# Attention backward: q for dK in 32 small pieces issued by the sync engine, three more buffers of transposed e, and dV four units later

## The chip, the cores and the metric

One core of a Trainium2 chip. The metric is device microseconds (us) of one execution; lower is better. A run more than 1.5% above the fastest of its kernel in the same rounds counts as slow and is left out of the ratios.

## The reference, cut to what matters

The program computes the forward of two attention layers and all eight gradients. The change touches the backward of layer B: softmax attention with 16 heads of 28 channels, 2048 queries and keys, and one k and one v shared by all heads.

```python
# x [1,2048,448]; wq [448,448]; wk, wv [448,28]; wo [448,448]; all bf16
q = (x @ wq).reshape(B, S, 16, 28).transpose(0, 2, 1, 3)
k = x @ wk                      # shared by the 16 heads
v = x @ wv
p = softmax(einsum("bhqd,bkd->bhqk", q, k) * 28 ** -0.5)
o = einsum("bhqk,bkd->bhqd", p, v)
# backward with dS = p * (dP - D):  dV = sum_h p^T dO, dK = sum_h dS^T q, dQ = dS k
```

Nine outputs: the forward and eight gradients.

## The kernel before

The main loop has 512 units. A block is 8 units: two heads and 256 queries against all 2048 keys, 64 blocks in all; a unit is 256 keys of it. A unit does 128x512 tiles twice: scores on PE, exp on ACT (eT, keys on partitions), the gradient product on DVE and, through a copy by ACT, on POOL (dsT), and a 32x32 transpose on DVE (dsx). After the 512 units come 28 of drain, then the projections of the gradients.

dV needs e with the queries on partitions. So every second unit the sync engine (SP) issues one DMA transpose of 512 KB, eN from eT: 256 in all. dK needs q with the queries on partitions (qX), four times over, at partitions 0, 32, 64 and 96. q lies in DRAM (qn_d); POOL fetches it for the next 8 blocks in four loads of 256 KB.

```python
pn_ = cs_.enter_context(tc.tile_pool(name="ceN", bufs=11, side="right"))
pq_ = cs_.enter_context(tc.tile_pool(name="cqX", bufs=2, side="right"))
# ... in the loop over u:
if u in (2, 4, 6, 8) or u % 64 in (30, 38, 46, 54) and u < 448:
    qc, a = (u // 64 + 1, (u % 64 - 30) // 8) if u > 20 else (0, (u - 2) // 2)
    if a == 0:
        qX[qc] = pq_.tile([P, 4, 2, 512], BF16, name="qX")
    nc.gpsimd.dma_start(qX[qc][32 * a:32 * a + 32, :, :, :]..., qn_d[qc * 256:(qc + 1) * 256, :]...)
if u == 4:
    nc.vector.memset(oTs[64:128, :], 0.0)
# ...
nc.scalar.activation(out=et[:, u % 2, 1, :], in_=sp[1][:, :], func=ACT.Exp, scale=scale)
if u % 2 == 1:
    en = pn_.tile([P, 16, P], BF16, name="eN")
    nc.sync.dma_start_transpose(en[:, :, :], et[:, :, :, :].rearrange("p a b c -> p (a b c)"))
    eN[u // 2] = en
if u % 2:
    b, i = divmod(u - 27, 8)          # dK of block b, units 8b+27 .. 8b+33
    ...
else:
    o_dq((u - 2, u - 1), (u - 20, u - 19))
    for n in {2: (0,), 4: (1, 2), 6: (3,)}.get(u % 8, ()):
        if 0 <= (b := u // 8 - 2) < NB:
            dv_mm(b, n // 2, n % 2)   # a quarter of dV: 4 matmuls of 512 columns
```

Of the kernel before, what the change touches and what calls it, by code (L numbers as in the profile page):

```python
# [11 lines left out]
BF16 = mybir.dt.bfloat16  # L12
F32 = mybir.dt.float32
# [3 lines left out]
D = 448  # L17
P = 128
# [6 lines left out]
def kernel(  # L25
# [21 lines left out]
    nc = tc.nc  # L47
    S = A_x.shape[1]
# [17 lines left out]
    R2 = R2x[:, 1:NS + 1, :]  # L66
    R3 = reg.tile([P, 4, 1408], BF16, name="R3")
    R4 = reg.tile([P, 4, 512], BF16, name="R4")
    qn_d = dpool.tile([S, 512], BF16, name="qn_d")
    on_d = dpool.tile([S, 512], BF16, name="on_d")  # L70
    wqT_d = dpool.tile([512, D], BF16, name="wqT_d")
    wkvT_d = dpool.tile([64, D], BF16, name="wkvT_d")
# [439 lines left out]
    def phase_B_pre(pa, cA, awk, psA, io):  # L512
        xbT, wq_pad, rep, bsel, qn, sh = io
        kT, vT, vaug, kn, qT = kT_rep, vT_rep, vaug_, kn_, R1

        def gen(shape, dt=F32):
            return psA.tile(shape, dt, name="agen")

        ones16 = cA.tile([P, H], BF16, name="ones16")
        nc.gpsimd.memset(ones16[:], 1.0)  # L520
        nc.gpsimd.memset(ones16[0:1, :], 0.0)
        neg = cA.tile([P, 1], F32, name="neg")
        nc.gpsimd.memset(neg[:], 0.0)
        for j in range(4):
            nc.gpsimd.memset(neg[32 * j:32 * j + 1, :], -1.0)
        kmx = cA.tile([H, NQC], F32, name="kmx")
        sqk = []
        def k_max(qc, sq):
            ps = gen([H, 512])
            mm(ps[:, :], ones16[0:32, :], sq[0:32, :])  # L530
            nc.vector.tensor_reduce(out=kmx[:, qc:qc + 1], in_=ps[:, :], axis=AX.X, op=ALU.max)

        prev = None
        for qc in range(NQC):
            for w, dst in [(0, kT), (1, vT)]:
                ps = gen([P, 512])
                for c in range(4):
                    mm(ps[:, :], rep[:, w, c, :], xbT[:, c, qc * 512:(qc + 1) * 512], start=(c == 0), stop=(c == 3))

                if w:  # L540
                    nc.vector.tensor_scalar(out=dst[:, qc * 512:(qc + 1) * 512], in0=ps[:, :], scalar1=neg[:, 0:1],
                                            scalar2=None, op0=ALU.add)
                else:
                    nc.scalar.activation(out=dst[:, qc * 512:(qc + 1) * 512], in_=ps[:, :], func=ACT.Identity,  # L544
                                         bias=neg[:, 0:1])
            sq = awk.tile([P, 512], BF16, name="osb")
            nc.vector.tensor_tensor(out=sq[0:32, :], in0=kT[0:32, qc * 512:(qc + 1) * 512],  # L547
                                    in1=kT[0:32, qc * 512:(qc + 1) * 512], op=ALU.mult)
            if prev is not None:
                k_max(qc - 1, prev)  # L550
            prev = sq
        shifts = [flat(sh)[0:H, i * 512:(i + 1) * 512] for i in range(NQC - 1)] + [flat(R3)[0:H, 5120:5632]]
        kmax2 = cA.tile([H, 1], F32, name="kmax2")
        for qc in range(NQC):
            qs = slice(qc * 512, (qc + 1) * 512)
            pn = psA.tile([P, 512], F32, name="aacc")
            sqs = []
            for g in range(6):
                if qc == 0 and g == 2:
                    k_max(NQC - 1, prev)  # L560
                    nc.vector.tensor_reduce(out=kmax2[:], in_=kmx[:], axis=AX.X, op=ALU.max)
                if g < 4:
                    ps = gen([P, 512])
                    for c in range(4):
                        mm(ps[:, :], wq_pad[:, c, g * P:(g + 1) * P], xbT[:, c, qs], start=(c == 0), stop=(c == 3))
                    nc.scalar.activation(out=qT[:, g, qs], in_=ps[:, :], func=ACT.Copy)
                    sq = awk.tile([P, 512], BF16, name="osb")
                    nc.vector.tensor_tensor(out=sq[:, :], in0=qT[:, g, qs], in1=qT[:, g, qs], op=ALU.mult)
                    sqs.append(sq)
                if g >= 2:  # L570
                    mm(pn[:, :], bsel[:, g - 2, :], sqs[g - 2][:, :], start=(g == 2), stop=(g == 5))
            shift = shifts[qc]
            nc.scalar.activation(out=shift, in_=pn[0:H, :], func=ACT.Sqrt, scale=kmax2[:, 0:1])
            for g in range(4):
                nc.gpsimd.dma_start(qT[:, g, qs].rearrange("(j r) s -> j r s", r=32)[:, 0, :], shift[4 * g:4 * g + 4, :])
            if qc % 2:
                q2 = slice((qc - 1) * 512, (qc + 1) * 512)
                t2 = slice(4 * qc - 4, 4 * qc + 4)
                for g in range(4):
                    nc.sync.dma_start_transpose(qn[:, t2, g * P:(g + 1) * P], qT[:, g, q2])  # L580
                nc.sync.dma_start(qn_d[q2, :].rearrange("(t p) c -> p t c", p=P), qn[:, t2, :])
        for w, dst in [(1, vaug_), (0, kn_)]:
            ps = gen([P, NS, 32])
            for st in range(NS):
                for c in range(4):
                    mm(ps[:, st, :], xbT[:, c, st * P:(st + 1) * P], rep[:, w, c, 0:32], start=(c == 0), stop=(c == 3))
            nc.vector.tensor_copy(out=dst, in_=ps[:])
        nc.gpsimd.memset(vaug_[:, :, 0:1], 1.0)
# [13 lines left out]
    NB = 64  # L602
# [4 lines left out]
    with ExitStack() as cs_:  # L607
        psA = psc.enter_context(tc.tile_pool(name="psAcc", bufs=1, space=bass.MemoryType.PSUM))
        pe_ = cs_.enter_context(tc.tile_pool(name="ceT", bufs=10, side="right"))
        pn_ = cs_.enter_context(tc.tile_pool(name="ceN", bufs=11, side="right"))  # L610
        pd_ = cs_.enter_context(tc.tile_pool(name="cdsT", bufs=5, side="right"))
        px_ = cs_.enter_context(tc.tile_pool(name="cdsx", bufs=2, side="right"))
        pq_ = cs_.enter_context(tc.tile_pool(name="cqX", bufs=2, side="right"))
# [45 lines left out]

        identF = pp_.tile([P, P], F32, name="identF", bufs=1)  # L660
        make_identity(nc, identF[:])
        oTs = pm_.tile([P, 256], F32, name="oTs", bufs=1)
        wo = pp_.tile([P, 4, D], BF16, name="wo", bufs=1)
        oTq = {}

# [32 lines left out]
            nc.scalar.activation(out=t, in_=src, func=ACT.Copy, scale=0.0)  # L698

        def post_load(k):  # L700
            if k in (2, 4, 6, 8):
                zero(post["dkvT"][64:128, 256 * k - 512:256 * k])
            if k == 0:
                mix = pq_.tile([P, 4, 2, 512], BF16, name="qX").rearrange("p a b c -> p (a b c)")
                post["dkvT"], post["dkvn"], post["wkvT"] = mix[:, 0:2048], mix[:, 2048:3072], mix[:, 3072:3072 + D]
                zero(post["wkvT"][64:128, :])
                nc.sync.dma_start(post["wkvT"][0:64, :], wkvT_d[:, :])
            i = k % 4
            rows = slice(i * 512, (i + 1) * 512)
            if k == 8:  # L710
                t = pe_.tile([P, 2, 2, 512], BF16, name="eT").rearrange("p a b c -> p (a b c)")
                post["wqT"] = t[:, 0:4 * D].rearrange("p (g c) -> p g c", c=D)
# [96 lines left out]
        def dk_m(b, m):  # L809
            qc, pair, g, hp = blk(b)  # L810
            h, B, s = m // 8, (m // 2) % 4, m % 2
            for a in range(4):
                rhs = dsx[b][32 * a:32 * a + 32, :, h, :, :].rearrange(
                    "p u t (b i s) -> p u t b i s", b=4, s=2)[:, :, :, B, :, s]
                mmt(dk_acc[32 * a:32 * a + 32, :],
                    qX[qc][32 * a:32 * a + 32, B, s, pair * 64 + 32 * h:pair * 64 + 32 * h + 32],
                    rhs, (32 * a, 32 * a), b == 0 and m == 0, b == NB - 1 and m == 15)

        def o_mm(v):
            b, tp = divmod(v, 8)  # L820
# [42 lines left out]
        with tc.manual_schedule():  # L863
            tc.keep_in_program_order(nc.scalar.activation(out=ex[:], in_=ex[:], func=ACT.Exp))
            for u in range(NU + 28):
# [23 lines left out]
                if hasD:  # L889
# [4 lines left out]
                    cp = pc_.tile([P, 512], BF16, name="cp")  # L894
                    nc.scalar.activation(out=cp[:, :], in_=dp[1][:, :], func=ACT.Copy)  # L895
                    nc.gpsimd.tensor_tensor(out=dst[:, 1, :], in0=cp[:, :], in1=ew[:, w % 2, 1, :], op=ALU.mult)  # L896
                if u in (2, 4, 6, 8) or u % 64 in (30, 38, 46, 54) and u < 448:
                    qc, a = (u // 64 + 1, (u % 64 - 30) // 8) if u > 20 else (0, (u - 2) // 2)
                    if a == 0:
                        qX[qc] = pq_.tile([P, 4, 2, 512], BF16, name="qX")  # L900
                    nc.gpsimd.dma_start(qX[qc][32 * a:32 * a + 32, :, :, :].rearrange("j b s c -> j b (s c)"),  # L901
                                        qn_d[qc * 256:(qc + 1) * 256, :].rearrange("(b j s) c -> j b (s c)", b=4, s=2))
                if u == 12:
                    nc.gpsimd.dma_start(wo, wo_d[:, 0:D].rearrange("(g p) c -> p g c", p=P))
                if u == 4:
# [25 lines left out]
                if hasS:  # L931
                    nc.scalar.activation(out=et[:, u % 2, 1, :], in_=sp[1][:, :], func=ACT.Exp, scale=scale)  # L932
                    if u % 2 == 1:
                        en = pn_.tile([P, 16, P], BF16, name="eN")
                        nc.sync.dma_start_transpose(en[:, :, :], et[:, :, :, :].rearrange("p a b c -> p (a b c)"))
                        eN[u // 2] = en

                if u % 2:
                    b, i = divmod(u - 27, 8)
# [2 lines left out]
                            dk_m(b, m)  # L942
                else:
                    o_dq((u - 2, u - 1), (u - 20, u - 19))
                    for n in {2: (0,), 4: (1, 2), 6: (3,)}.get(u % 8, ()):
                        if 0 <= (b := u // 8 - 2) < NB:
                            dv_mm(b, n // 2, n % 2)
                y = u - 18

                if 512 <= u < 530 and u % 2 == 0:  # L950
# [117 lines left out]
```

## Time and profile before

| | before |
|---|---|
| three timed runs, us | 1121.45, 1121.01, 1111.03 |
| profiled run: span, mean clock | 1111.3 us, 0.994 |
| first start of a transpose of e to the last | 802.7 us (235.3 to 1038.0) |

### The profile page before, as it was taken

Reading aid. Unit: us, or ns where it says so; the run is one execution under the profiler, and the core shown is the slowest. Engines: PE = TensorE matmul, PEld = TensorE weight load, DVE = VectorE, ACT = ScalarE, POOL = GpSimd, SP = SyncE. Lnnn points to the kernel's source line nnn. Section 1 sums busy time; section 2 is a strip of 40 time slices with the busy share of each in tenths; the row PEclk is TensorE's granted clock in tenths of the full one; section 3 lists DMA queues with packets and bytes.
Section 4 is the critical chain, followed back from the end, with each engine's and each line's share of the span. In section 5 each row is a group of like instructions: output and inputs, shape, how many; then the busy total and the mean of one; then the engine's idle time right before and its main releaser. Section 6 shows DMA issues by size and latency. Waiting matters only on the chain.

```text
span 1111.3 us, 42443 instructions
## 1 busy us (share of the span) xinstructions
PE 1047.9 (94%) x17280; PEld 503.6 (45%) x17285; DVE 893.8 (80%) x1773; ACT 876.6 (79%) x1744; POOL 768.7 (69%) x993
## 2 busy tenths in 40 slices
PE   9999999969999999999999999999999999999898
PEld 4545545435444444444444444444444444444344
DVE  7896400427999999999999999999999999999842
ACT  6454122548999999999999999999999999999521
POOL 6001252325888898898889888888898888888740
PEclk9999999979999999999999999999999999999999
DMA  9869899199999999999999999999999999999992
GB/s 264 147 128 185 166 174 222 43 202 198 177 167 184 195 196 177 187 189 187 191 186 199 191 183 197 195 188 178 191 193 180 195 182 194 192 184 184 237 212 62
DMA packets 674963, 202.89 MB, mean 183 GB/s; under 512 B 649760, under 2 KB 670288, under 8 KB 674768
## 3 DMA queue, kind: packets, MB, share of 16 engines
q1 hardware_dynamic: 662368, 177.03, 100.1%
q0 software_dynamic: 7440, 19.20, 6.7%
q10 hardware_dynamic: 4960, 3.96, 1.2%
q8 instruction: 135, 2.21, 0.8%
q14 instruction: 60, 0.49, 0.2%
HBM read 22.83 MB, written 14.77 MB: 34 GB/s over the span
## 4 chain that ended last, share of the span: by engine, by line
PE 65%; DVE 12%; DMA 10%; ACT 9%; issue 2%; SPq 1%; POOL 0%; DVEq 0%; ACTq 0%
PE dk_acc L627 18%; PE agen L81 12%; PE sps L627 11%; DMA eN<-eT 8%; ACT eT L932 7%; PE oq L627 6%; PE dps L627 5%; PE aacc L81 4%; DVE dsT L893 4%; PE dv_acc L627 3%; DVE dsx L964 3%; PE sps L81 3%; PE sps L800 1%; ACT cp L895 1%; DVE R L916 1%
## 5 line engine op out<-in xcount | busy, mean ns | idle before, releaser
L896 POOL TENSOR_TENSOR dsT<-cp,eT 128x512 bf16<-128x512 bf16 x512 | 590.0, 1157 | 108.7 <-ACT cp L895 96.8
L893 DVE TENSOR_TENSOR dsT<-dps,eT 128x512 bf16<-128x512 f32 x512 | 341.4, 667 | 27.9 <-PE dps L627 22.1
L627 PEld LDWEIGHTS <-R 32*128 32x128 bf16 (+1 forms) x8704 | 228.5, 94 | 296.7 <-issue 263.0
L964 DVE STREAM_TRANSPOSE dsx<-dsT 128x512 f32<-128x512 f32 x512 | 356.0, 696 | 2.1
L888 ACT ACTIVATE eT<-sps 128x512 bf16<-128x512 f32 x512 | 312.5, 610 | 42.8 <-PE dps L627 19.0
L895 ACT ACTIVATE cp<-dps 128x512 bf16<-128x512 f32 x512 | 313.5, 612 | 12.9 <-PE dps L627 11.9
L932 ACT ACTIVATE eT<-sps 128x512 bf16<-128x512 f32 x512 | 320.1, 625 | 0.0
L627 PE MATMUL dk_acc<-dsx,qX 32*32 32x512 bf16 x4096 | 268.0, 376 | 0.0
L627 PE MATMUL dps<-doT,R 32*128 32x256 bf16 x2048 | 248.0, 269 | 6.1 <-ACT cp L895 2.0
L627 PE MATMUL sps<-R,R 32*128 32x256 bf16 (+1 forms) x2240 | 226.4, 274 | 8.6 <-DVE R L858 1.9
L627 PE MATMUL oq<-eT,R 128*32 128x256 bf16 x2048 | 158.3, 275 | 0.0
L627 PE MATMUL oq<-dsT,R 128*32 128x256 bf16 x2048 | 156.4, 274 | 0.1
L627 PEld LDWEIGHTS <-qX 32*32 32x32 bf16 x4096 | 79.8, 89 | 114.5 <-issue 54.1
L627 PE MATMUL dv_acc<-eN,don 128*32 128x512 bf16 x1024 | 103.0, 379 | 9.9 <-DMA eN<-eT 9.7
L397 POOL MEMSET ga<- 64x448 bf16 x2 | 0.9, 470 | 93.4 <-DVE pr L348 80.4
L547 DVE TENSOR_TENSOR osb<-R 32x512 bf16<-32x512 bf16 x4 | 1.7, 414 | 63.1 <-ACT R L544 63.1
L81 PEld LDWEIGHTS <-R 128*128 128x128 bf16 (+1 forms) x361 | 29.5, 99 | 27.5 <-issue 5.6
L627 PE MATMUL sps<-identF,oTs 128*32 128x64 f32 x1024 | 27.6, 225 | 7.5 <-ACT eT L932 0.2
L627 PEld LDWEIGHTS <-don 128*32 128x32 bf16 x1024 | 34.4, 97 | 0.3
L774 POOL TENSOR_TENSOR onat<-oTs,rl 128x128 bf16<-128x128 f32 x64 | 25.7, 402 | 6.5 <-DVE rl L770 6.5
L901 POOL DMA_DIRECT2D qX<-qn_d x32 | 18.6, 581 | 16.5 <-DMA qn_d<-gaT 16.5
L81 PE MATMUL agen<-R,R 128*128 128x448 bf16 x128 | 28.6, 353 | 0.8 <-ACT R L220 0.6
(225 smaller groups left out, 1029.1 us busy)
## 6 DMA issues: line engine op xcount, KB each, us to landing
qX<-qn_d POOLq DMA_DIRECT2D x32, 256.0 KB, 5.5
eN<-eT SPq DMA_TRANSPOSE x256
out_dram<-osb ACTq DMA_DIRECT2D x22, 112.0 KB
qn_d<-gaT SPq DMA_DIRECT2D x2, 1024.0 KB
xa<-in_A_x_dram SPq DMA_DIRECT2D x8, 224.0 KB
ga<-in_grad_out_dram SPq DMA_DIRECT2D x4, 448.0 KB
xa<-in_grad_out_dram POOLq DMA_DIRECT2D x4, 448.0 KB, 8.9
out_dram<-wdq POOLq DMA_DIRECT2D x8, 224.0 KB, 5.2
```

The source lines that it names most:

```text
L81: nc.tensor.matmul(out_ap, lhsT=lhsT, rhs=rhs, start=start, stop=stop, tile_position=(0, 0))
L627: nc.tensor.matmul(out, lhsT=lhsT, rhs=rhs, start=start, stop=stop, tile_position=pos, skip_group_check=True)
L774: nc.gpsimd.tensor_tensor(out=onv, in0=os_, in1=r_[:].to_broadcast([P, 2, 2, 32]), op=ALU.mult)
L800: nc.tensor.transpose(tp2[q:q + 32, qb * P:(qb + 1) * P], don[b][:, qb, h, :], identB[:, :], tile_position=(0, q))
L888: nc.scalar.activation(out=et[:, u % 2, 0, :], in_=sp[0][:, :], func=ACT.Exp, scale=scale)
L893: nc.vector.tensor_tensor(out=dst[:, 0, :], in0=dp[0][:, :], in1=ew[:, w % 2, 0, :], op=ALU.mult)
L895: nc.scalar.activation(out=cp[:, :], in_=dp[1][:, :], func=ACT.Copy)
L896: nc.gpsimd.tensor_tensor(out=dst[:, 1, :], in0=cp[:, :], in1=ew[:, w % 2, 1, :], op=ALU.mult)
L901: nc.gpsimd.dma_start(qX[qc][32 * a:32 * a + 32, :, :, :].rearrange("j b s c -> j b (s c)"), qn_d[qc * 256:(qc + 1) * 256, :].rearrange("( ...
L916: nc.vector.tensor_scalar(out=qT_B[g][64 * hp:64 * hp + 64, qc * 256:(qc + 1) * 256], in0=oq[64:128, 0:256], scalar1=scale, scalar2=None, ...
L932: nc.scalar.activation(out=et[:, u % 2, 1, :], in_=sp[1][:, :], func=ACT.Exp, scale=scale)
L964: nc.vector.transpose(out=dsx[b][:, tp, :, :, :].rearrange("p h t c -> p (h t c)").bitcast(F32), in_=dsT[y][:, :, :].rearrange("p h c -> p ...
```

## The change

Its intent: give dV more slack against late transposes (due four units later, one quarter per even unit, and 14 buffers in place of 11 to keep eN that long). The room comes from q, held in pieces of four heads (2 KB per partition, not 8). That makes 32 pieces of four loads of 64 KB; all but the first two pieces are now issued by SP, between transposes. oTs also moves to another pool.

```diff
-    qn_d = dpool.tile([S, 512], BF16, name="qn_d")
+    qn_d = dpool.tile([4, S, P], BF16, name="qn_d")
@@ before the loop: two stores of 1 MB become eight of 256 KB
-        pn_ = cs_.enter_context(tc.tile_pool(name="ceN", bufs=11, side="right"))
+        pn_ = cs_.enter_context(tc.tile_pool(name="ceN", bufs=14, side="right"))
-        oTs = pm_.tile([P, 256], F32, name="oTs", bufs=1)
+        oTs = pp_.tile([P, 256], F32, name="oTs", bufs=1)
@@ new
+        def load_q(k, a, eng):
+            qc, g = divmod(k, 4)
+            if a == 0:
+                qX[k] = pq_.tile([P, 4, 2, P], BF16, name="qX")
+            eng.dma_start(qX[k][32 * a:32 * a + 32, :, :, :]..., qn_d[g, qc * 256:(qc + 1) * 256, :]...)
@@ in the loop
-                if u in (2, 4, 6, 8) or u % 64 in (30, 38, 46, 54) and u < 448:
-                    ... nc.gpsimd.dma_start(qX[qc]...)
+                if 2 <= u < 10:
+                    load_q((u - 2) // 4, (u - 2) % 4, nc.gpsimd)
@@ after the transpose of e, odd u
+                    k, a = divmod(u - 11, 16)
+                    if 2 <= k < 32 and a < 4:
+                        load_q(k, a, nc.sync)
@@ even u
-                    for n in {2: (0,), 4: (1, 2), 6: (3,)}.get(u % 8, ()):
-                        if 0 <= (b := u // 8 - 2) < NB:
-                            dv_mm(b, n // 2, n % 2)
+                    b, n = divmod(u - 22, 8)
+                    if 0 <= b < NB:
+                        dv_mm(b, n // 4, n // 2 % 2)
```

(Cut: the tiles of the drain, which took a q buffer before and now take eN buffers. The four loads of piece k are emitted one per unit, at units 16k+11 to 16k+14.)

More of the change, by code (lines that the diff above doesn't have):

```diff
@@ L580, in phase_B_pre @@
                     nc.sync.dma_start_transpose(qn[:, t2, g * P:(g + 1) * P], qT[:, g, q2])
-                nc.sync.dma_start(qn_d[q2, :].rearrange("(t p) c -> p t c", p=P), qn[:, t2, :])
+                    nc.sync.dma_start(qn_d[g, q2, :].rearrange("(t p) c -> p t c", p=P), qn[:, t2, g * P:(g + 1) * P])
         for w, dst in [(1, vaug_), (0, kn_)]:
@@ L700, in post_load @@
         def post_load(k):
-            if k in (2, 4, 6, 8):
-                zero(post["dkvT"][64:128, 256 * k - 512:256 * k])
-            if k == 0:
-                mix = pq_.tile([P, 4, 2, 512], BF16, name="qX").rearrange("p a b c -> p (a b c)")
-                post["dkvT"], post["dkvn"], post["wkvT"] = mix[:, 0:2048], mix[:, 2048:3072], mix[:, 3072:3072 + D]
+            if 5 <= k < 9:
+                zero(post["dkvT"][64:128, 512 * k - 2560:512 * k - 2048])
+            i = k % 4
+            rows = slice(i * 512, (i + 1) * 512)
+            if k == 4:
+                post["dkvT"], mix = (pn_.tile([P, 16, P], BF16, name="eN").rearrange("p a b -> p (a b)") for _ in range(2))
+                post["dkvn"], post["wkvT"] = mix[:, 0:1024], mix[:, 1024:1024 + D]
                 zero(post["wkvT"][64:128, :])
                 nc.sync.dma_start(post["wkvT"][0:64, :], wkvT_d[:, :])
-            i = k % 4
-            rows = slice(i * 512, (i + 1) * 512)
             if k == 8:
@@ L815, in dk_m @@
                 mmt(dk_acc[32 * a:32 * a + 32, :],
-                    qX[qc][32 * a:32 * a + 32, B, s, pair * 64 + 32 * h:pair * 64 + 32 * h + 32],
+                    qX[b // 2][32 * a:32 * a + 32, B, s, hp * 64 + 32 * h:hp * 64 + 32 * h + 32],
                     rhs, (32 * a, 32 * a), b == 0 and m == 0, b == NB - 1 and m == 15)
+        def load_q(k, a, eng):
+            qc, g = divmod(k, 4)
+            if a == 0:
+                qX[k] = pq_.tile([P, 4, 2, P], BF16, name="qX")
+            eng.dma_start(qX[k][32 * a:32 * a + 32, :, :, :].rearrange("j b s c -> j b (s c)"),
+                          qn_d[g, qc * 256:(qc + 1) * 256, :].rearrange("(b j s) c -> j b (s c)", b=4, s=2))
         def o_mm(v):
@@ L896 @@
                     nc.gpsimd.tensor_tensor(out=dst[:, 1, :], in0=cp[:, :], in1=ew[:, w % 2, 1, :], op=ALU.mult)
-                if u in (2, 4, 6, 8) or u % 64 in (30, 38, 46, 54) and u < 448:
-                    qc, a = (u // 64 + 1, (u % 64 - 30) // 8) if u > 20 else (0, (u - 2) // 2)
-                    if a == 0:
-                        qX[qc] = pq_.tile([P, 4, 2, 512], BF16, name="qX")
-                    nc.gpsimd.dma_start(qX[qc][32 * a:32 * a + 32, :, :, :].rearrange("j b s c -> j b (s c)"),
-                                        qn_d[qc * 256:(qc + 1) * 256, :].rearrange("(b j s) c -> j b (s c)", b=4, s=2))
+                if 2 <= u < 10:
+                    load_q((u - 2) // 4, (u - 2) % 4, nc.gpsimd)
                 if u == 12:
```

## The prediction

> **What bounds the kernel now.** I read the busy table first, then the stretches of the main loop (512 units, one 128x512 score pair each, then 28 units of drain), then the waits, then the timeline around the longest of them. Two stretches of the loop (columns: window, length, then busy us of PE, weight load, DVE, ACT, POOL, clock, DMA share, GB/s):
>
> ```profile
> 600.00:700.00 100.00, 95.44 (x1931) 44.58 (x1929) 96.37 (x186) 98.10 (x197) 88.95 (x105) 1.00 1.20 190
> 700.00:800.00 100.00, 93.47 (x1853) 42.92 (x1852) 92.74 (x177) 94.17 (x189) 86.07 (x103) 1.00 1.19 189
> ```
>
> Four engines are above 86%: they are coupled through three score banks and two gradient banks, and where nothing disturbs them ACT reaches 98%. The second window is worse by 2 to 4 us on every engine at once, so something outside them stops all of them. The waits over the loop name two candidates:
>
> ```profile
> ACT eT L888 <- PE sps L627: 17.8, 12, 9.8
> DVE dsT L893 <- PE dps L627: 17.8, 35, 1.9
> POOL qX L901 <- DMA qn_d<-gaT: 16.5, 1, 16.5
> DVE oTs L906 <- DMA qn_d<-gaT: 9.9, 1, 9.9
> PE dv_acc L627 <- DMA eN<-eT: 9.7, 10, 1.7
> ```
>
> First, PE waits ten times for the transposed e (eN) that dV reads. The timeline of the longest wait shows what one costs:
>
> ```profile
> 526.66 0.39 PE L627 MATMUL dv_acc<-eN,don 128*32 128x512 bf16 x3
> ...
> 528.71 0.38 PE L627 MATMUL dv_acc<-eN,don 128*32 128x512 bf16 x1 [1.66 <-DMA eN<-eT]
> ...
> 529.45 0.60 ACT L888 ACTIVATE eT<-sps 128x512 bf16<-128x512 f32 x1 [2.06 <-PE dps L627]
> 529.49 0.69 DVE L893 TENSOR_TENSOR dsT<-dps,eT 128x512 bf16<-128x512 f32 x1 [1.86 <-PE dps L627]
> ```
>
> Three of the four matmuls ran, the fourth waited for the last eN of its block, and ACT and DVE then stood 2 us because the next scores sit behind it in PE's order. I took the starts of the second exp of all 512 units: the step is 1.43 us after odd units and 1.5 to 1.7 after even ones (class medians, sum 12.24 us per block of 8 units). Ten later steps stand out (2.2 to 3.7 us), all at u mod 8 = 2, where dV's first quarter is issued. Above their class median of 1.65 they hold 13.3 us in all.
>
> Second, at the start:
>
> ```profile
> 244.40 0.27 DVE L906 MEMSET oTs<- 64x256 f32 x1 [9.85 <-DMA qn_d<-gaT]
> 247.64 0.60 ACT L888 ACTIVATE eT<-sps 128x512 bf16<-128x512 f32 x1 [9.85 <-PE sps L627]
> 244.82 2.23 POOL L901 DMA_DIRECT2D qX<-qn_d  x4 [16.52 <-DMA qn_d<-gaT]
> ```
>
> A memset of oTs stands in DVE's order until q has been stored, and ACT stops for 9.85 us. By the tile sizes oTs lies where the natural q (gaB) was: on the right side the pools before it take 150,912 bytes per partition, gaB covers 137,380 to 153,764.
>
> Why is eN late? The SP queue that issues the transposes:
>
> ```profile
> L935 SPq DMA_TRANSPOSE eN<-eT x256: 1334/2987/6579, 235.3 to 1038.0; - x128
> ```
>
> 256 issues of 2.99 us mean are 766 of the 805 us between first and last. SP is never ahead: from the end of an odd unit's second exp to the start of its transpose pass 6.7 us at least, 9.7 at the median, and to landing 15.6 us (10 units). dV's first quarter comes 11 units after the last transpose of its block is emitted, so the margin is one unit. Over units 80 to 500 a transpose starts every 3.10 us; four engines undisturbed need 12.24/4 = 3.06. DMA and engines are bounds of nearly equal height, and every hiccup of one hits the other.
>
> **What the Trainium skill says.** "Perfetto Trace Analysis", Per-instruction lifecycle, HWDGE: the shown span of such an issue holds the use of the descriptor generator, data movement lies outside, and engines start early when descriptors exceed the buffer. That fits: issues range from 1.33 to 5 us, about 2,000 packets of 256 B start during each, and an issue ends about when the transpose before it lands. I read the 2.99 us as waiting for room, not as SP's own work. "DMA: Bandwidth & Descriptors", Latency and other measured facts, gives 261 GB/s for a DMA transpose with a non-contiguous middle dimension; here 512 KB per 2.76 us in blocks without other traffic is 190 GB/s, so the trace is lower. The same page, Issuing engines are not separate DMA queues: another issuer saves only issue time. The trace agrees: transposes around a POOL load of q average 3.1 us, those away from any 2.65 to 2.8, about 1.3 us of DMA per 256 KB. Its Specifications ask for 512 B per transfer for line rate; the new loads are just that, and the new stores of q fall to 256 B.
>
> **The change, part by part.**
> - *dV four units later, one quarter per even unit.* No work is removed: 1024 matmuls stay. The last eN of a block is now due 15 units after its emission, 4 x 1.53 = 6.1 us more. The double quarter at u mod 8 = 4 goes to u mod 8 = 0. PE's sum per block is unchanged; I book 0 to -3 us for evenness over the loop. With 14 buffers a block's eN lives from 8b+1 to 8b+28, exactly 14 pairs, so no new wait for a buffer. The stalls: 13.3 us; I expect two thirds to go, -9 us, since a slower DMA stream still eats margin.
> - *oTs moved.* Its new pool begins beyond gaB (155,008), so the 9.85 us memset wait goes. Not all is gained: POOL still waits for the stores of q (244.2), then issues 8 loads instead of 4 (8 x 0.56 = 4.5 us, to 248.7), then needs the 2.2 us from onat to the finished don (253.60 to 255.75 before). So don is ready at about 250.9 instead of 255.75: -5 us.
> - *q in 32 pieces of 4 loads.* 28 POOL issues of 0.58 us go (POOL is no bound: 0). 120 SP issues of 64 KB come. A plain issue on SP shows 0.36 to 0.54 us when free; 4 per 8 transposes are 1.8 us per 24.7 us. If SP's spans are waiting for room, this lies beneath the drain. Data: packets of 896 B on this queue take 44 to 48 ns, of 256 B 18 to 27; I estimate 33 ns for 512 B, so 16,384 packets over 16 engines are 34 us. Before, 2,496 packets of 257 ns were 40 us. Net 0, with -10 to +20 us as its spread.
> - *Stores of q by head group, later post-load tiles:* 8 stores of 256 KB instead of 2 of 1 MB; the last must land before POOL starts, which may shift the start by 2 us either way. The drain keeps its dK end at unit 537; dV ends at 532 instead of 526. 0 to +1 us.
>
> Sum: -9 - 5 - 1 = -15 us from the profiled run's 1113.0, so 1098. The timed runs reach 1121, and runs with more stalls should gain more, so I keep 1098 as the median.
>
> **Rivals.**
> 1. *The DMA stream is the true bound.* Then later dV buys one shift (about 6 us) and the start some 6 us for SP, which waited for exps of units 7 and 9; nothing in between. For it: SP's continuous backlog. Against: undisturbed stretches run for 60 us without a stall. Time: about 1101.
> 2. *The loads on SP take real SP time.* 120 x 0.5 = 60 us of issue in a queue with 5% free would slow the transposes to about 3.2 us and the kernel to 1115 to 1125. A form of it: dK now waits. Piece k is needed at unit 16k+27, its last load is emitted at 16k+14, 13 units, less than dV's 15. At today's 10 units to landing it holds; at 13 PE stalls on q instead of eN.
> 3. *All stalls vanish and evenness helps.* Units at 1.50 to 1.51 us, ACT at 99%: 512 x 0.03 = 15 us more, so 1083 to 1087.
> 4. *The start gains nothing* because q's smaller stores land late: 1103.
>
> **Range and chances.** The four cases span 1083 to 1125; the middle ones are likelier, so 1083 to 1115 for 8 in 10. The comparison base is between 1113 and 1121 by the timed runs; 2% below is 1091 to 1099, just about my estimate, hence nearly even chances between faster and same: 0.42 and 0.53. Slower by 2% needs rival 2 in full: 0.05.
>
> **What would show it.** Right: no DVE wait on oTs, ACT's gap at unit 6 gone with a shorter one near units 10 to 14; dV's waits on eN near zero; steps at u mod 8 = 2 back to 1.65; transposes still about 3.0 us apart. Wrong: waits of dk_acc for a transfer of qX, transposes 3.2 us apart or more, a longer wait at the start, or a unit step that stays at 1.53 with eN margins that shrink to zero late in the loop.

## More of the kernel before

The stretches, waits and timelines that matter are in the prediction. Beside them, two rows of the costliest groups and two of the DMA issues. In the first two the columns after the bar are busy time, mean ns of one, and idle time before them with what ended most of it; in the last two, count, size and (where known) us from issue to landing.

```profile
L627 PE MATMUL dk_acc<-dsx,qX 32*32 32x512 bf16 x4096 | 268.0, 376 | 0.0
L627 PE MATMUL dv_acc<-eN,don 128*32 128x512 bf16 x1024 | 103.0, 379 | 9.9 <-DMA eN<-eT 9.7
...
qX<-qn_d POOLq DMA_DIRECT2D x32, 256.0 KB, 5.5
eN<-eT SPq DMA_TRANSPOSE x256
```

dV waits now and then for a transpose, dK never for q. All transposes are issued by SP, all loads of q by POOL.

Output 6 is the gradient of B's wk.

## The result, and the profile after

Ratios here are the mean time of one kernel's fast runs over the mean of the other's in the same rounds, so not quite the ratio of the medians quoted. The first result's ratio rests on two of the four runs of the kernel before (1111.03 and 1104.41); over all four it would be 1.025. Later rounds have the kernel before at medians of 1111.2 to 1117.3, so the loss is some 2.3 to 3.1%, slower in every reading.

| | before | after |
|---|---|---|
| median, us | 1116.02 (1104.41 to 1121.45, 4 runs) | 1142.88 (1140.77 to 1143.78, 4 runs) |
| ratio | | **1.0315**, interval 1.0257 to 1.0372: slower |
| profiled span, mean clock | 1111.3 us, 0.994 | 1141.1 us, 0.972 |
| start of the first transpose of e to that of the last | 802.7 us | 828.0 us |
| transposes 40 to 250: one starts every | 3.103 us | 3.245 us |
| end of exp to landing of its transpose, median | 15.6 us | 19.7 us |

The prediction of 1098 was wrong, and its range up to 1115 too low.

From the page of the kernel after, the rows that answer to those shown above:

```profile
L627 PE MATMUL dk_acc<-dsx,qX 32*32 32x512 bf16 x4096 | 283.9, 384 | 20.5 <-DMA qX<-qn_d 20.5
L627 PE MATMUL dv_acc<-eN,don 128*32 128x512 bf16 x1024 | 111.4, 386 | 0.0
...
qX<-qn_d SPq DMA_DIRECT2D x120, 64.0 KB
```

The change did what it was made for: dV's waits for eN went from 9.7 us to zero. But dK, which never waited, now waits 20.5 us for q. The same two stretches of the loop as in the prediction (columns as there):

```profile
600.00:700.00 100.00, 92.12 (x1772) 40.98 (x1772) 89.56 (x171) 91.25 (x182) 81.17 (x96) 0.95 1.12 184
700.00:800.00 100.00, 92.67 (x1844) 41.93 (x1836) 91.84 (x176) 93.72 (x188) 82.74 (x97) 0.97 1.14 182
```

The first is down on DVE and ACT by 7 us, and 96 POOL instructions in place of 105 say how much less work was passed through. The waits of the loop (window 300 to 1050; columns: total us, times, longest):

```profile
DVE dsT L900 <- PE dps L627: 37.6, 45, 4.3
PEld L627 <- DMA qX<-qn_d: 25.5, 17, 3.4
ACT eT L895 <- issue: 24.2, 11, 4.6
...
PE dk_acc L627 <- DMA qX<-qn_d: 20.5, 14, 3.1
```

PE stops for q, and ACT and DVE stop behind it, up to 4.6 us at a time. The second and the fourth line are two sides of partly the same stops (PE's weight load needs q first), so they aren't added. One of PE's longest waits, in the SP, PE and ACT timelines (columns: start, us, what, and in brackets the idle time before it):

```profile
880.29 1.01 SPq L823 DMA_DIRECT2D qX<-qn_d  x2
881.40 3.26 SPq L938 DMA_TRANSPOSE eN<-eT  x1
884.71 1.44 SPq L823 DMA_DIRECT2D qX<-qn_d  x2
```

```profile
884.32 0.39 PE L627 MATMUL dk_acc<-dsx,qX 32*32 32x512 bf16 x2
887.55 2.42 PE L627 MATMUL dk_acc<-dsx,qX 32*32 32x512 bf16 x14 [2.84 <-DMA qX<-qn_d]
```

```profile
890.59 0.60 ACT L895 ACTIVATE eT<-sps 128x512 bf16<-128x512 f32 x1 [4.60 <-issue]
```

SP issues the last two loads of the piece from 884.71 to 886.15; PE, whose next dK matmul was due at 884.71, goes on at 887.55. So the load is late because SP got to it late. The piece is needed at unit 16k+27 and its last load is emitted 13 units earlier, some 20 us; from emission to landing these last loads took 19.0 us at the median and 22.5 at most, most of it standing in line behind transposes.

The two kinds of instruction in that line, by tile (columns: ns minimum/median/maximum, first and last start):

```profile
L938 SPq DMA_TRANSPOSE eN<-eT x256: 1315/2852/5088, 239.2 to 1067.2; - x128
```

```profile
L823 SPq DMA_DIRECT2D qX<-qn_d x120: 313/478/1937, 308.4 to 1066.7; - x120
```

From here the account is by SP. Over the 802.7 us (before) and 828.0 us (after) of its stretch of transposes:

| SP's time, us | before | after | difference |
|---|---|---|---|
| 256 transposes | 763.6 | 702.4 | -61.2 |
| 120 loads of q | 0 | 75.3 | +75.3 |
| gaps between instructions | 21.6 | 29.7 | +8.1 |
| other (the whole less the above) | 17.5 | 20.6 | +3.1 |
| stretch | 802.7 | 828.0 | **+25.3** |

The span grew by 29.8 us. Of that the loop from its first exp to its last took 20.2 more (801.9 to 822.1), and 9.9 came after the last exp (the first exp was 0.3 earlier), where the queue's backlog is worked off: the last transpose starts 16.2 us after the last exp, 6.9 before. SP's loads of the stored o stand behind it, and PE stops for them (1.5 us before):

```profile
1075.09 1.68 PE L81 MATMUL sps<-eT,eN 128*128 128x448 bf16 x4 [8.81 <-DMA eN<-on_d]
```

At the start the memset of oTs no longer waits (it runs at 234.30, not 244.40), and POOL issues eight loads in place of four:

```profile
247.42 4.39 POOL L823 DMA_DIRECT2D qX<-qn_d  x8 [19.42 <-DMA qn_d<-gaT]
```

```profile
256.49 0.60 ACT L895 ACTIVATE eT<-sps 128x512 bf16<-128x512 f32 x1 [4.25 <-PE sps L627]
```

POOL comes free at 251.8 and finishes the first don at 254.0, against 255.75 before. The first 64 units take 103.4 us, 106.3 before.

### The profile page after: what moved, and what is told of

Read it like the earlier page. It is cut to its first block, busy times and chain, and to the rows that moved or that the text cites. A ratio compares the mean times of both kernels' runs of the same rounds, so it can differ in the third digit from the quotient of the medians.

```text
span 1141.1 us, 42580 instructions
## 1 busy us (share of the span) xinstructions
PE 1060.0 (93%) x17285; PEld 501.0 (44%) x17285; DVE 895.8 (79%) x1773; ACT 879.3 (77%) x1744; POOL 754.9 (66%) x969
## 4 chain that ended last, share of the span: by engine, by line
PE 60%; DVE 18%; ACT 10%; DMA 5%; issue 3%; POOL 2%; SPq 1%; DVEq 0%; ACTq 0%; POOLq 0%
PE dk_acc L627 17%; PE agen L81 12%; PE sps L627 10%; ACT eT L935 7%; DVE dsT L900 7%; DVE dsx L970 6%; PE oq L627 5%; PE aacc L81 4%; PE dps L627 4%; PE sps L81 3%; DMA qX<-qn_d 3%; PE dv_acc L627 2%; DVE R L919 2%; ACT cp L902 2%; POOL dsT L903 1%
## 5 line engine op out<-in xcount | busy, mean ns | idle before, releaser
L627 PEld LDWEIGHTS <-R 32*128 32x128 bf16 (+1 forms) x8704 | 220.9, 95 | 288.8 <-issue 263.6
L627 PE MATMUL dk_acc<-dsx,qX 32*32 32x512 bf16 x4096 | 283.9, 384 | 20.5 <-DMA qX<-qn_d 20.5
L627 PE MATMUL dps<-doT,R 32*128 32x256 bf16 x2048 | 250.9, 273 | 15.7 <-DVE dsT L900 12.2
L627 PE MATMUL oq<-eT,R 128*32 128x256 bf16 x2048 | 161.6, 280 | 0.1
L627 PE MATMUL oq<-dsT,R 128*32 128x256 bf16 x2048 | 159.2, 277 | 0.1
L627 PEld LDWEIGHTS <-qX 32*32 32x32 bf16 x4096 | 84.3, 90 | 144.5 <-issue 59.5
L627 PE MATMUL dv_acc<-eN,don 128*32 128x512 bf16 x1024 | 111.4, 386 | 0.0
L919 DVE TENSOR_SCALAR R<-oq 64x256 bf16<-64x256 f32 x64 | 27.3, 427 | 4.8 <-PE oq L627 2.8
L627 PEld LDWEIGHTS sps<-identF,oTs 128*32 128x32 f32 x1024 | 17.2, 109 | 25.3 <-ACT eT L935 25.0
```

Source lines behind the costliest of these rows:

```text
L627: nc.tensor.matmul(out, lhsT=lhsT, rhs=rhs, start=start, stop=stop, tile_position=pos, skip_group_check=True)
L919: nc.vector.tensor_scalar(out=qT_B[g][64 * hp:64 * hp + 64, qc * 256:(qc + 1) * 256], in0=oq[64:128, 0:256], scalar1=scale, scalar2=None, ...
```

## The experiments

The theory after the first look: SP's queue sets the pace of the loop, and each load takes real time of it, whatever it carries. Rivals: (a) the data, 1 MB per 64 units in 512-byte packets, not the issues; (b) the late piece: dK's margin of 13 units, with the queue only the place where it shows; (c) dV's new places; (d) the half-clock stretches behind PE's stops. All of the twelve runs follow. "Stream" is the time from the first transpose's start to the last's.

| | median us | ratio to before [95%] | stream us | loads of q in it, by | result |
|---|---|---|---|---|---|
| after | 1142.9 | 1.0315 [1.0257, 1.0372] | 828.0 | 120 x 64 KB, SP | correct |
| e1_fixed_q | 1096.2 | 0.9831 [0.9769, 0.9893] | 776.7 | none | wrong |
| e2_tiny_sp | 1131.2 | 1.0145 [1.0083, 1.0206] | 818.0 | 120 x 1 KB, SP | wrong |
| e3_pool_q | 1117.4 | 1.0020 [0.9952, 1.0089] | 807.5 | 120 x 64 KB, POOL | correct |
| e4_ots_only | 1114.6 | 1.0003 [0.9929, 1.0077] | 801.1 | 28 x 256 KB, POOL | correct |
| e5_sp32 | 1110.4 | 0.9988 [0.9927, 1.0048] | 797.2 | 28 x 256 KB, SP | correct |
| e6_sp32_ots | 1112.3 | 1.0002 [0.9948, 1.0056] | 799.6 | 28 x 256 KB, SP | correct |
| e7_q_early | 1139.4 | 1.0238 [1.0178, 1.0298] | 823.2 | 120 x 64 KB, SP | correct |
| e8_dv_old | 1140.7 | 1.0254 [1.0198, 1.0309] | 825.3 | 120 x 64 KB, SP | correct |
| e9_tiny_60 | 1112.8 | 1.0000 [0.9962, 1.0038] | 796.9 | 60 x 1 KB, SP | wrong |
| e10_sp_all | 1109.5 | 0.9968 [0.9927, 1.0009] | 800.3 | 32 x 256 KB, SP | correct |
| e11_piece8 | 1124.9 | 1.0104 [1.0063, 1.0145] | 812.4 | 64 x 128 KB, SP | correct |
| e12_ots_fixed | 1092.2 | 0.9807 [0.9758, 0.9855] | 777.7 | none | wrong |

The four wrong ones leave pieces of q out, so output 6 is wrong (relative error 1.35); the other outputs are as in a correct run.

**e1_fixed_q: after, without the 120 loads.** Later pieces reuse the first two.

```diff
-                    if 2 <= k < 32 and a < 4:
-                        load_q(k, a, nc.sync)
+                    if 2 <= k < 32 and a == 0:
+                        qX[k] = qX[k % 2]
```

> The changed kernel, but q is loaded only for the first two pieces and those are used for every block (dK and what follows from it are wrong on purpose); no load of q is issued on SP in the loop. Theory A (the 120 loads in SP's queue slow the stream of transposes and come late themselves) and B (it is their bytes, in packets of 512 B, not their place in SP's queue): no wait of dk_acc, transposes 2.8 to 3.0 us apart instead of 3.245, 1085 to 1100 us. Theory C (dV's new placement or the new layout is what costs): stays at 1125 us or more.

Measured: 1096.2 us. The loads cost 47 us by the medians. All other parts of the change are still in this run (dV, buffers, oTs, the stores, the drain), so none of them costs the time by itself. The queue is now ahead: a transpose starts 0.1 us after its exp at the median (transposes 40 to 250; 14.0 in the kernel after). ACT shows what the loop can do (window 300 to 1000: busy us of PE, weight load, DVE, ACT, POOL):

```profile
300.00:1000.00 700.00, 667.04 (x13696) 309.57 (x13696) 677.70 (x1301) 689.32 (x1377) 608.14 (x708) 1.00 1.17 183
```

ACT is busy 98.5%: here the engines are the bound. This run does not say which side of a load costs, issue or data.

**e2_tiny_sp: the same number of issues, almost no data.** As e1, with a dummy load of 1 KB in each of the 120 places.

```diff
+                    if 2 <= k < 32 and a < 4:
+                        tiny = pp_.tile([32, 16], BF16, name="tiny", bufs=4)
+                        nc.sync.dma_start(tiny, qn_d[k % 4, k // 4 * 256:k // 4 * 256 + 32, 0:16])
```

> As e1, but at the places of the 120 loads SP issues loads of 32 rows of 32 B into a tile that nobody reads: the issue and the place in the queue without the bytes (1 KB instead of 64 KB; dK wrong on purpose). A in its form of issue cost: transposes 3.15 to 3.25 us apart, 1115 to 1140 us. B: within 5 us of e1, transposes below 3.0 us apart.

Measured: 1131.2 us, 35 of the 47 us lost again with 1/64 of the data and nothing in the kernel waiting for it.

```profile
L938 SPq DMA_TRANSPOSE eN<-eT x256: 1315/2696/6295, 238.6 to 1056.6; - x128
```

```profile
L945 SPq DMA_DIRECT2D tiny<-qn_d x120: 407/569/2063, 308.5 to 1056.0; - x120
```

The 120 tiny loads take 74.0 us of SP, as much as the real ones (75.3), while the transposes beside them are no faster than 2.71 us mean. Rival (a) is left with some 12 us, rival (b) can't be the main cause, since no dK waits for a tiny load. The wait moves to the other reader of the queue: dV waits 16.1 us for eN in the loop.

**e3_pool_q: the same loads, issued by POOL.**

```diff
-                        load_q(k, a, nc.sync)
+                        load_q(k, a, nc.gpsimd)
```

> The changed kernel with one edit: the 120 loads of q are issued on POOL instead of SP, same bytes, same packets, same units; result right. A: no wait of dk_acc for qX, transposes 3.0 to 3.1 us apart, 1090 to 1110 us, unless POOL, which gets 120 x 0.58 = 70 us of issue more, becomes the bound (then 1110 to 1120 with POOL above 95% in the loop). B: the bytes still contend, transposes above 3.15 us apart, 1120 us or more.

Measured: 1117.4 us, 25 less than after, with the same data in the same pieces. So the issuer alone accounts for most of the loss. But not because SP is rid of 75 us: its transposes take 768.4 us in this run, 66.0 more than in the kernel after, slowed beside the loads on POOL's queue as in the kernel before. Of the 20.5 us by which the stream is shorter, 9.3 come from this exchange and 11.2 from fewer gaps and other entries in SP's queue. Window and waits of the loop:

```profile
300.00:1000.00 700.00, 654.41 (x13416) 294.99 (x13412) 666.76 (x1276) 679.62 (x1351) 652.81 (x810) 1.00 1.20 187
```

```profile
PEld L800 <- POOL don L792: 29.6, 54, 0.8
```

POOL is busy 93% (the fifth figure, 608 in e1), and PE waits for don, which POOL makes: the unit step at u mod 8 = 6 is 1.73 us (1.53 in e1), so a block takes 12.48 us (12.28). The queue is slower still, 4 x 3.163 = 12.65 us, so its lag behind the exps grows from some 5 us to 16, and PE stops 9.3 us for the stored o at the end. Why e3 doesn't beat before is therefore both, POOL in the loop and the queue at its end; no run separates them.

**e4_ots_only: before, with oTs moved, nothing else.**

```diff
-        oTs = pm_.tile([P, 256], F32, name="oTs", bufs=1)
+        oTs = pp_.tile([P, 256], F32, name="oTs", bufs=1)
```

> The kernel before with oTs alone moved to the last pool. Prediction's part: DVE's 9.85 us wait on the memset goes and ACT's gap at unit 6 with it, 5 us less in the first 16 units; over the whole kernel 3 to 6 us less if engines bound the loop, and as little as 0 to 2 us if the stream of transposes sets the end.

Measured: 1114.6 us, ratio 1.0003. The 9.85 us wait is gone and the time is the same. The start of the loop shows where it went, PE first, then ACT:

```profile
259.42 0.59 PE L627 MATMUL dv_acc<-eN,don 128*32 128x512 bf16 x1 [4.85 <-DMA eN<-eT]
```

```profile
262.27 0.60 ACT L888 ACTIVATE eT<-sps 128x512 bf16<-128x512 f32 x1 [7.36 <-PE dps L627]
```

The exps run ahead and then stop 7.4 us at unit 18, where the first dV waits for its transposes: SP had not been freed earlier. The first 64 units even take 108.4 us (106.3 before).

**e5_sp32 and e6_sp32_ots: before's 28 loads of 256 KB, issued by SP; e6 with oTs moved as well.**

```diff
-                    nc.gpsimd.dma_start(qX[qc][32 * a:32 * a + 32, :, :, :]...
+                    (nc.sync if u > 20 else nc.gpsimd).dma_start(qX[qc][32 * a:32 * a + 32, :, :, :]...
```

> The kernel before with one edit: its 28 loads of q in the loop (256 KB, all 16 heads) are issued on SP instead of POOL; nothing else. If what costs is the number of issues in SP's queue, 28 x 0.6 = 17 us are cheap, and with POOL's queue silent the transposes should take 2.7 instead of 2.95 us each: (2.73 + 0.06 + 0.07 + 0.04) = 2.9 us apart against 3.06 that the engines need, so SP is no longer behind, dV's waits for eN go, 1096 to 1106 us. If any plain load in SP's queue hurts, or its bytes do: 1112 to 1125 us.

> e5 and oTs in the last pool. With SP no longer the bound the 5 us of the start should now come through: 3 to 6 us less than e5. If the start gives it back, as in e4: within 2 us of e5.

Measured: 1110.4 and 1112.3 us, no difference from before, and so not the gain that e5 was expected to bring if the count alone costs. Nearly all the bytes of the change (7.2 MB of 7.7, in larger packets) cost no more on SP's queue than on POOL's when they come in 28 issues (17.7 us of SP) in place of 120. It gains nothing either: SP's transposes shrink from 2.95 to 2.87 us mean, and the loads take that up (0.073 us per transpose).

**e7_q_early: after, with q 16 units earlier** (three qX buffers, 13 of eN, dV two units earlier to fit).

```diff
-                    k, a = divmod(u - 11, 16)
+                    k, a = divmod(u + 5, 16)
```

> The changed kernel with three buffers of q and each piece loaded 16 units earlier (13 buffers of eN, dV 20 to 26 units behind, to make room); still 120 loads on SP. If the late arrival of q is the cause: no wait of dk_acc and 1100 to 1112 us. If the pace of SP's queue is the cause and dK's wait only the place where it shows: no wait of dk_acc, but transposes still 3.15 to 3.25 us apart, dV waiting for eN (or ACT for eT) in its place, 1125 to 1142 us.

Measured: 1139.4 us, 3.5 less than after, and the intervals of the two ratios overlap. The waits for q are gone, and dV waits instead:

```profile
PE dv_acc L627 <- DMA eN<-eT: 31.0, 29, 2.3
```

So rival (b) falls: dK's waits were where the queue's lateness showed, not a cause. One reader relieved, the next one waits.

**e8_dv_old: after, with dV in its old places.**

```diff
-                    b, n = divmod(u - 22, 8)
-                    if 0 <= b < NB:
-                        dv_mm(b, n // 4, n // 2 % 2)
+                    for n in {2: (0,), 4: (1, 2), 6: (3,)}.get(u % 8, ()):
+                        if 0 <= (b := u // 8 - 2) < NB:
+                            dv_mm(b, n // 2, n % 2)
```

> The changed kernel with dV back at 18 to 22 units behind, in quarters 1, 2, 1 as before. If SP's pace sets the time: dV takes over the waits from dK, its margin being 11 units instead of 15, and the time rises little, 1143 to 1155 us. If the later dV itself costs: below 1135 us.

Measured: 1140.7 us against 1142.9: rival (c) falls too. The later dV is worth nothing that shows; with it undone, dV waits 25.7 us for eN in the loop and dK no longer for q.

**e9_tiny_60: e2 with 60 tiny loads** (`a in (0, 2)` in place of `a < 4`), to see whether the cost goes with the count.

> e2 with half of its tiny loads (60 in place of 120). If SP's queue costs only where it is slower than the engines (a threshold): SP could then give a transpose every 2.73 + 0.11 + 0.04 + 60 x 0.62 / 256 = 3.03 us, just under the 3.06 of the engines, so most of e2's loss is gone, 1096 to 1108 us. If each load costs alike: the middle of e1 and e2, 1110 to 1117 us.

Measured: 1112.8 us. The stream is 20 us longer than with none (e1) and the one with 120 (e2) is 41 longer: it goes with the count. The time does not go with it in the same way. From first exp to last e9 takes 790.3 us, only 3.9 more than e1, and e2 23.6 more. In e9 the queue is just slower than the engines: its lag grows from some 4 us to 16 over the loop without stopping dV much (2.0 us in all), and the rest of the loss, 12 us, is paid at the end, where PE stops 9.6 us for the stored o that SP loads after its backlog (10.4 in e2). The 60 loads take 43.4 us of SP, 0.72 each.

**e10_sp_all: e6, with the first four loads on SP too** (at units 10 to 13), so that POOL makes don sooner.

```diff
-                if u in (2, 4, 6, 8) or u % 64 in (30, 38, 46, 54) and u < 448:
+                if u in (10, 11, 12, 13) or u % 64 in (30, 38, 46, 54) and u < 448:
```

> e6 with the first four loads of q on SP too, at units 10 to 13, so that POOL no longer waits at the start for q's stores. ACT's gaps in units 6 to 20 shrink by 4 to 8 us. If engines set the time after that: 1103 to 1108 us. If SP's pace (3.11 us per transpose in e6) sets it, the start is given back as in e4: 1108 to 1113 us.

Measured: 1109.5 us, ratio 0.9968 [0.9927, 1.0009]. The start is 5.4 us shorter (first 64 units 100.9), and the stream is 800.3 us, as in e6: the time saved at the start is spent behind the queue. Nominally the best correct version, but its interval holds 1, so it is not called faster.

**e11_piece8: after, with q in 16 pieces of eight heads**, loads of 128 KB, emitted earlier (13 eN buffers, dV two units earlier).

> The changed kernel with pieces of eight heads: 64 loads of 128 KB on SP, spread over units and 19 units or more ahead of their use, 13 buffers of eN, dV 20 to 26 units behind, first piece on SP too. Per 32 units SP has 16 transposes of 2.73 and 4 loads of 0.63 with 512 KB that take some 2.7 us to drain: 3.0 to 3.1 us per transpose, about the engines' 3.06, with two units more of slack for dV than before: 1097 to 1108 us, faster than both. If the queue is still behind: 1110 us or more with dV's waits back.

Measured: 1124.9 us, between after and before, as is the stream. With the first piece's four loads SP issues 64, which take 48.3 us: 0.75 each, 0.63 for the 64 KB ones. Half the issues give back 18 of 27 us, though this version also loads earlier and stores q in four parts, not eight, so the 18 us are not the count's alone. It is not the gain over before that was hoped for: dV waits 24.5 us for eN.

**e12_ots_fixed: e4 without its 28 loads in the loop.** Before's dV, before's 11 buffers, no loads.

```diff
+                if u % 64 == 30 and u < 448:
+                    qX[u // 64 + 1] = qX[0]
-                if u in (2, 4, 6, 8) or u % 64 in (30, 38, 46, 54) and u < 448:
+                if u in (2, 4, 6, 8):
```

> e4 (the kernel before with oTs moved) without its 28 loads of q in the loop: the first piece serves all blocks (dK wrong on purpose). dV stays 18 to 22 units behind in quarters 1, 2, 1 with 11 buffers. If the stream of transposes bounds the kernel before, and its loads of q are a part of that stream: transposes no more than 3.06 us apart, no backlog, dV's waits gone, 1095 to 1102 us, within 5 us of e1; then the later dV and its three buffers are worth next to nothing by themselves. If the later dV is worth something: 1103 to 1112 us, with dV's waits for eN still there.

Measured: 1092.2 us, nominally 4 less than e1 (the intervals of the two ratios overlap). This is what decides the worth of the change's intended half: with no loads at all, the late dV and its three buffers (e1) do no better than the old ones (e12). And it shows before's own bound: 28 loads by an engine with time to spare cost 22 us (1.93% of 1117), and the transposes are slower beside them (2.95 us mean with them, 2.76 without). The run takes issues and data away together; that it is not POOL's issue time follows from e5, where POOL is free of them and nothing is gained.

```profile
L937 SPq DMA_TRANSPOSE eN<-eT x256: 1327/2893/7413, 234.7 to 1012.4; - x128
```

Two further versions were not run: one load per piece that writes all four copies, and e7 with 14 eN buffers.

## Why the prediction was wrong, by its steps

**What held.** Rival 2 named the mechanism: loads that take SP's time, transposes about 3.2 us apart (3.245), dK waiting for q because 13 units are less than dV's 15. So did rival 1, the DMA stream as the true bound, though not its time of 1101. Rival 2 was right and was given too little: 1115 to 1125 for a measured 1142.9, and a chance of 0.05 for slower. The memset wait on oTs went, dV's waits for eN went, POOL was no bound, and the packets of 512 B were sized about right (36.6 ns mean, 33 estimated).

**The step that failed** is "If SP's spans are waiting for room, this lies beneath the drain", with its "Net 0". I took the 2.99 us of a transpose on SP as mostly waiting, into which another issue could slip. The runs: 120 issues took 75.3 us (0.63 each; rival 2 had 0.5 each, so 60). The transposes shrank by 61 us, which looks like slipping in, but most of that, 0.19 x 256 = 49 us, came with the end of POOL's large loads: e12, with no loads at all, has 2.76 us per transpose where before and e4 have 2.95 and 2.94. e2 adds 0.31 us of tiny loads per transpose, and it falls only to 2.71. So at most 0.05 of 0.31 us fits beneath, and the rest lengthens the queue. (Against e1, which is e2 without the loads, nothing fits: 2.60 us there, though in a queue that is often idle.) The step was not without ground: right behind a pair of tiny loads, 1.25 us together, a transpose takes 2.33 us and the others 2.83. But the queue as a whole hardly got that back. Stream: 777 us without loads, 803 with before's 28 on POOL, 828 with 120 on SP.

Why the total is the stream: in the kernels whose queue is behind throughout, span less stream is 308 to 314 us, before and after alike (316 in e9). The 25.3 us of the stream are most of the span's 29.8; the other 4.5 lies ahead of the first transpose (3.9 us, 239.2 against 235.3) and in the tail.

**The second failed step** is the booking of -9 us for dV's stalls and -5 us for the start. Before was already bound by the queue: SP started each transpose 6.7 us or more after its exp (transposes 40 to 250), which I had read and written down. Where a queue is this far behind, its reader's stalls are the form in which its pace reaches the engines. Taking a stall away moves it: from the oTs memset to unit 18 (e4), from dK to dV (e7), from dV to dK (e8 the other way round), from the start to the middle (e10). None moved the time beyond its interval. The start itself gained 2.9 us in its first 64 units, not 5: POOL could begin its loads only at 247.42, not at the 244.2 of the sum, since it waited longer for the stores of q (rival 4, in part). Evenness of dV, 0 to -3 in the sum, is 0: an undisturbed block takes 12.28 us with the new dV (e1) and 12.24 with the old (e12), by the class medians of the unit steps.

**A hit that means nothing.** e1 ran in 1096 us, near the predicted 1098, but e12 reaches 1092 without the change's dV. The 15 us I predicted were there to be had, from having no loads of q, not from the parts I credited.

**Data or issues.** e2 against after (10 us of stream) is what the data cost on top of the issues; e5 says that before's 28 loads, issue and data together, cost about the same on either issuer, and e12 puts that at some 22 us. So both sides count, and they overlap. That large loads cost mainly by their data and small ones by their number fits these runs; large loads without data were not run.

**What stays open.** Why a transpose of 512 KB holds SP for 2.60 us even in e1, without loads, by building its descriptors or by waiting until they drain, is not settled; only that a plain issue hardly fits beneath it. The traces lean to waiting for a part of it: in the kernel before, transposes whose predecessor landed 1.5 to 2.0 us after their start took 1.92 us (36 of them), those whose predecessor landed 4.0 to 4.5 us after took 3.69 (28). The half-clock stretches (rival (d): around the 2.84 us stop above the clock was halved for 6.8 us) were not separated by a run of their own. The loop of the kernel after has seven, 37.5 us in all, before has none. But e7 has two, 6.8 us, and e8 five, 17.1, and both are within 4 us of after, so they are not the main part.

## What to carry to other kernels

Before adding work to a queue, find out whether it is ever ahead: compare each issue's start with the end of what produces its data, not only its busy share. If it is always behind, its pace is the kernel's pace: the lag stalls its readers or, as in e9, is paid after the loop. Stalls of its readers are then symptoms, and more slack or more buffers for one reader only pass the stall to the next. For small transfers count issues, not bytes: here 120 loads of 1 KB cost most of what 120 of 64 KB did, and 28 of 256 KB on the same queue cost no more than on POOL's.

## What the Trainium skill lacked or had wrong

- "DMA: Bandwidth & Descriptors", Issuing engines are not separate DMA queues, calls the issue time that another issuer saves "usually small relative to the DMA itself". Here it weighed more: with the same 120 loads on POOL (e3) in place of SP the kernel is 25 us of 1143 faster, and 120 loads of 1 KB (e2) took 74 us of SP.
- "Perfetto Trace Analysis", Per-instruction lifecycle, says that the sequencer is free for its next instruction only at the end of the shown span. The runs agree, and the prediction read past it: 0.31 us of other issues per transpose shortened a transpose's span only from 2.76 (e12) to 2.71 us (e2). What it does not say is how the span divides between building descriptors and waiting for room: spans run from 1.31 to 5.09 us in the kernel after, all for transposes of 512 KB.
- "TensorE: Matmul & The Clock Gate", Part 1, puts the half clock after at least one idle window of about 3.4 us, and calls the window free-running. The traces agree with the window: the seven half-clock stretches in the loop of the kernel after start whole multiples of 3.413 us apart. But the window need not be idle. In the stop shown above PE ran until 884.71 and the clock fell at 886.13; in the 3.41 us before that PE was busy 1.87. Between 260 and 1060 us of all 14 traces, cut at this grid, all 21 full-clock windows with PE busy below half were followed by half clock and none above 58%; between these 10 were and 11 were not (PE's ends are modelled, so the limits are rough). The 1.66 us stop in the prediction's timeline is one that was not: PE busy 1.98 of 3.41 us, granted 1.00 over 528.70 to 532.00. Three stretches of the kernel after, with the stop in the first and half clock from 886.13 to 892.96 (the clock is third from the end):

```profile
880.00:887.50 7.50, 4.59 (x114) 2.15 (x102) 6.04 (x13) 5.81 (x12) 6.14 (x8) 0.91 0.75 160
887.50:892.50 5.00, 4.95 (x54) 1.51 (x58) 1.50 (x3) 1.58 (x4) 0.75 (x1) 0.50 1.13 205
892.50:900.00 7.50, 7.20 (x147) 3.43 (x145) 7.01 (x13) 7.31 (x15) 5.77 (x8) 0.97 1.15 188
```
